# PV of a unit and scores of the next in one place on TensorE, with q/k transposes two units ahead

## The chip, the cores and the metric

The kernel runs on one core of a Trainium2 chip. The metric is device time in microseconds of one execution; lower is better. The engines are named as the profile names them: PE (TensorE matmul; PEld its weight loads), ACT (ScalarE), DVE (VectorE), POOL (GpSimd), SP (SyncE, which here only issues DMAs).

## What is computed

Chunked attention, then a two-layer network on the 4608 tokens that it gives. Batch 8, 8 heads, sequence 576, head size 64; attention stays inside chunks of 64 tokens.

```python
scores = scale * np.matmul(q_c, k_c.transpose(0, 1, 2, 4, 3))   # per chunk of 64
attn = np.exp(scores - max); attn = attn / (sum(attn) + 1e-09)
x = np.matmul(attn, v_c)              # -> x: 4608 tokens x 512
h = x @ w_in                          # 512 -> 2048
g = h * (1.0 / (1.0 + np.exp(-beta * h)))
out = g @ w_out                       # 2048 -> 512, float32
```

## The kernel before, in words

**Tiling.** The 4608 tokens are cut into 18 units of 256 tokens (four chunks, all heads) and 9 blocks of two units (512 tokens). Block j holds units 2j and 2j + 1. Matrices are in fp16, sums in fp32 PSUM.

**A unit's way.** `load_unit` has POOL issue the DMAs of q, k and v (fp32 in DRAM, converted on the way). `emit_T(u)` brings k and q into the layout with head size on partitions; from unit 8 on (`XU = 8`) these are two DMA transposes issued by SP (L149), before that transposes on DVE. `emit_T` also asks for the loads of unit u + 4 (`loads_to`), whose q and k go into the four-buffer pool `qk` that this T reads. `emit_sc(u)` puts the scores into the two banks of the PSUM pool `ps_s` with 32 small matmuls (64 x 64, four at a time on the array; L218) and ACT takes their exponential (L224). `emit_pv(u)` makes the product with v, the sum of the exponentials as a 65th column, in two halves of 16 small matmuls (L256): half 0 in `ps_x`, half 1 in `ps_s`. `emit_norm(u, s)` divides on DVE (reciprocal L267, multiply L271), and `emit_xt_dma(u, s)` has SP transpose the half into the block's tile `xt` (L292).

**A block's two layers.** `emit_m(j, m)`, m from 0 to 15, is one slice of the first layer: four matmuls of 512 columns into one bank of `ps_p` called `hps` (L303), then tanh on ACT (L313) and a multiply-add on DVE (L317) that writes `gt`. It reads the whole `xt` tile of its block, all four transposed halves. `emit_t(j, t, k0, k1)` is the second layer for 128 tokens: 16 matmuls of 512 columns into one bank called `ops` (L335), in two halves of eight; after the second, ACT copies it out (L345) and SP issues the DMA to DRAM (L347).

**PSUM.** Eight banks: four in `ps_p`, handed out in turn, two in `ps_s`, two in `ps_x`.

**The order.** Nothing reorders instructions: the program runs under `tc.manual_schedule()`, and each engine executes in the order in which the code emits. SP and POOL are such queues too. Blocks 0 to 2 are written out by hand. For blocks 3 to 8 a list of items with due times is sorted: 16 `emit_m`, 8 halves of `emit_t` of the block before (j - 1), and the attention of the two units of the next block:

```python
items.append((0.98 * (t + 0.5 * hf) / 4, 1, ("t", t, hf)))
return [(a0, 2, ("sc", u)), (a0 + 0.40 * w, 3, ("pv", u)),
        (a0 + 0.41 * w, 3, ("norm", u, 0)), (a0 + 0.55 * w, 3, ("norm", u, 1)),
        (a0 + 0.10 * w, 3, ("T", u + 1))]
```

So a block begins with a half of `ops`, then two `hps`, then the next half of `ops`, and so on; scores of a unit, its PV and the scores of the next unit stand at three different places among them, and the transposes of unit u + 1 follow the scores of unit u. In the profile of before, block 3 begins at 97.27 us, block 4 at 126.83, block 8 at 245.04.

Of the kernel before, what the change touches and what calls it, by code (L numbers as in the profile page):

```python
# [8 lines left out]
FP32 = mybir.dt.float32  # L9
FP16 = mybir.dt.float16  # L10
ACTF = mybir.ActivationFunctionType
ALU = mybir.AluOpType
# [3 lines left out]
def kernel(  # L16
# [10 lines left out]
    nc = tc.nc  # L27
    B, H, S, D = q.shape
# [4 lines left out]
    KFF = DFF // 128  # L33
    UNIT = 256
    NU = NT // UNIT
# [4 lines left out]
    const = ctx.enter_context(tc.tile_pool(name="const", bufs=1))  # L40
    big = ctx.enter_context(tc.tile_pool(name="big", bufs=1))
    qk_p = ctx.enter_context(tc.tile_pool(name="qk", bufs=4))
    qt_p = ctx.enter_context(tc.tile_pool(name="qt", bufs=2))
    et_p = ctx.enter_context(tc.tile_pool(name="et", bufs=3))
    rd_p = ctx.enter_context(tc.tile_pool(name="rd", bufs=2))
    x_p = ctx.enter_context(tc.tile_pool(name="x16", bufs=4))
# [4 lines left out]
    ps_p = ctx.enter_context(tc.tile_pool(name="ps_p", bufs=4, space=bass.MemoryType.PSUM))  # L51
    ps_s = ctx.enter_context(tc.tile_pool(name="ps_s", bufs=1, space=bass.MemoryType.PSUM))
    ps_x = ctx.enter_context(tc.tile_pool(name="ps_x", bufs=1, space=bass.MemoryType.PSUM))
# [112 lines left out]
    et_t = {}  # L166
# [39 lines left out]
    def emit_ex(u):  # L206
        ex_t[u].pop(0)()

    def emit_sc(u, split=False, later=False):
        qt, kt = qT.pop(u), kT.pop(u)  # L210
        sc = ps_s.tile([128, 2, H, CH], FP32, tag="s", name="sc")
        if u >= XU:
            qx, kx = (t.rearrange("p h s e -> p (h s e)").rearrange("p (j c t) -> p j c t", j=H, c=2)
                      for t in (qt, kt))
            for jj in range(H):
                for par in range(2):
                    for c in range(2):
                        nc.tensor.matmul(  # L218
                            out=sc[64 * c:64 * c + 64, par, jj, :],
                            lhsT=kx[64 * par:64 * par + 64, jj, c, :],  # L220
                            rhs=qx[64 * par:64 * par + 64, jj, c, :],
                        )
            et = et_p.tile([128, 2, H, CH], FP16, tag="et", name="et")
            nc.scalar.activation(out=et, in_=sc, func=ACTF.Exp, scale=scale)  # L224
            et_t[u] = et
            return
        for h in range(H):
            for e in range(2):
                for c in range(4):
                    p0, o0 = 32 * c, 64 * (c % 2)  # L230
                    nc.tensor.matmul(  # L231
                        out=sc[o0:o0 + 64, c // 2, h, :],
                        lhsT=kt[p0:p0 + 32, h, :, e],
                        rhs=qt[p0:p0 + 32, h, :, e],
                        start=(e == 0),
                        stop=(e == 1),
                    )
        et = et_p.tile([128, 2, H, CH], FP16, tag="et", name="et")
        ex_t[u] = [
            lambda s=s: nc.scalar.activation(out=et[:, s], in_=sc[:, s], func=ACTF.Exp, scale=scale)  # L240
            for s in ([0, 1] if split or later else [slice(0, 2)])
        ]
        et_t[u] = et
        while ex_t[u] and not later:
            emit_ex(u)

    def emit_pv(u):
        et = et_t.pop(u)
        for s in range(2):
            i = 2 * u + s  # L250
            pool, tag = ((ps_x, "x"), (ps_s, "s"))[s]
            x = pool.tile([128, 2, 4, 128], FP32, tag=tag, name="x")
            for g in range(4):
                for r in range(2):
                    for c in range(2):
                        nc.tensor.matmul(  # L256
                            out=x[64 * c:64 * c + 64, r, g, 0:D + 1],
                            lhsT=(et[64 * r:64 * r + 64, s, 4 * c + g, :] if u < XU else
                                  et[64 * r:64 * r + 64, g % 2, 4 * s + 2 * c + g // 2, :]),
                            rhs=vbig[64 * r:64 * r + 64, i, 4 * c + g, 0:D + 1],  # L260
                        )
            x_t[u, s] = x

    def emit_norm(u, s):
        x = x_t.pop((u, s))
        rd = rd_p.tile([128, 2, 4, 1], FP32, tag="rd", name="rd")
        nc.vector.reciprocal(out=rd, in_=x[:, :, :, D:D + 1])  # L267
        x16 = x_p.tile([128, 2, 4, D], FP16, tag="x16", name="x16")
        for r in ([0, 1] if u < 2 else [slice(0, 2)]):
            o = x16[:, r]  # L270
            nc.vector.tensor_tensor(  # L271
                out=o, in0=x[:, r, :, 0:D], in1=rd[:, r].to_broadcast(list(o.shape)), op=ALU.mult
            )
        x16_t[u, s] = x16
# [15 lines left out]
    def emit_xt_dma(u, s):  # L290
        xf = x16_t.pop((u, s)).rearrange("p r h d -> p (r h d)")
        nc.sync.dma_start_transpose(out=xt_at(u, s), in_=xf)  # L292
# [3 lines left out]
    def emit_m(j, m, c0=0, n=None, later=False):  # L296
        n = blocks[j][1] * UNIT if n is None else n
        if j not in gt_t:
            gt_t[j] = gt_p.tile([128, KFF, 512], FP16, tag="gt", name="gt")
        hps = ps_p.tile([128, 512], FP32, tag="p", name="hps")  # L300
        xr = xt_t[j].rearrange("p t (r k) (c q) -> p (t r) (k c) q", r=2, c=2)
        for kk in range(KDM):
            nc.tensor.matmul(  # L303
                out=hps[:, 0:n],
                lhsT=w_in16[m // 2][:, kk, (m % 2) * 128:(m % 2) * 128 + 128],
                rhs=xr[:, c0 // CH:(c0 + n) // CH, 2 * (kk % 2) + kk // 2, :],
                start=(kk == 0),
                stop=(kk == KDM - 1),
            )
        sg = sg_p.tile([128, 512], FP32, tag="sg", name="sg")  # L310

        def act():
            nc.scalar.activation(  # L313
                out=sg[:, 0:n], in_=hps[:, 0:n], func=ACTF.Tanh, scale=beta2[:, m:m + 1])

        def vec():
            nc.vector.scalar_tensor_tensor(  # L317
                out=gt_t[j][:, m, c0:c0 + n], in0=sg[:, 0:n], scalar=1.0, in1=hps[:, 0:n],
                op0=ALU.add, op1=ALU.mult,
            )  # L320

        if later:
            return act, vec
        act()
        vec()
# [3 lines left out]
    def emit_t(j, t, k0=0, k1=None):  # L329
        k1 = KFF if k1 is None else k1  # L330
        if k0 == 0:
            ops_t[j, t] = ps_p.tile([128, DM], FP32, tag="p", name="ops")
        ops = ops_t[j, t]
        for kk in range(k0, k1):
            nc.tensor.matmul(  # L335
                out=ops,
                lhsT=gt_t[j][:, kk, t * 128:(t + 1) * 128],
                rhs=w_out16[kk // 4][:, kk % 4, :],
                start=(kk == 0),
                stop=(kk == KFF - 1),  # L340
            )
        if k1 < KFF:
            return
        osb = osb_p.tile([128, DM], FP32, tag="osb", name="osb")
        nc.scalar.activation(out=osb, in_=ops, func=ACTF.Copy, scale=0.5)  # L345
        r0 = blocks[j][0] * UNIT + t * 128
        nc.sync.dma_start(out=out[r0:r0 + 128, :], in_=osb)  # L347
# [6 lines left out]
    with tc.manual_schedule():  # L354
# [149 lines left out]
                emit_xt_dma(7, 1)  # L504
                loads_to(11)

        def att_items(u, a0, w):
            return [(a0, 2, ("sc", u)), (a0 + 0.40 * w, 3, ("pv", u)),
                    (a0 + 0.41 * w, 3, ("norm", u, 0)), (a0 + 0.55 * w, 3, ("norm", u, 1)),
                    (a0 + 0.10 * w, 3, ("T", u + 1))]  # L510

        for j in range(3, NB):
            items = [(0.02 + 0.98 * m / KFF, 0, ("m", m)) for m in range(KFF)]
            for t in range(4):
                for hf in range(2):
                    items.append((0.98 * (t + 0.5 * hf) / 4, 1, ("t", t, hf)))
            if j + 1 < NB:
                for i in range(2):
                    items += att_items(2 * j + 2 + i, 0.03 + 0.43 * i, 0.43)
            items.sort(key=lambda it: it[:2])  # L520
            for _, _, it in items:
                if it[0] == "m":
                    emit_m(j, it[1])
                elif it[0] == "t":
                    emit_t(j - 1, it[1], 8 * it[2], 8 * it[2] + 8)
                elif it[0] == "sc":
                    emit_sc(it[1])
                elif it[0] == "pv":
                    emit_pv(it[1])
                elif it[0] == "norm":  # L530
                    emit_norm(it[1], it[2])
                    emit_xt_dma(it[1], it[2])
                elif it[1] < NU:
                    emit_T(it[1])
        for t in range(3):
            emit_t(NB - 1, t)
        for hf in range(2):
# [47 lines left out]
```

The softmax here doesn't subtract the row's maximum and nothing guards it: scores larger than these inputs give would overflow.

## Time and profile before

| | |
|---|---|
| median of 3 runs | 291.93 us (291.70 to 292.49) |
| the profiled execution | 291.74 us, span 290.0 us |
| PE busy | 283.1 us (98%), granted clock 1.0 |
| ACT / DVE busy | 146.0 us (50%) / 139.8 us (48%) |
| first layer, PE L303 | 608 matmuls, mean 368 ns |
| second layer, PE L335 | 560 matmuls, mean 379 ns |
| DMA queue of POOL, q0 | 101216 packets, 18.10 MB |
| DMA queue of SP, q1 | 40544 packets, 18.24 MB |
| unit's load of q (128 KB a DMA), issue to landing | median 6.6 us |
| transposes of k / q from unit 8 on, issue to landing | median 7.2 / 9.8 us |
| transposes into xt, issue to landing | median 3.5 us |

The span runs from the first to the last instruction; the time of an execution has 1.7 us more around it. Ends of matmuls are modelled and overlap the next one's start, so PE's pace is read from starts: eight matmuls of 512 columns take 1.727 us from start to start. Busy shares are means over the span; what an edit is worth is read at its own place in the timeline.

### The profile page before, as it was taken

How to read it: one execution, taken by the hardware profiler on the slowest of the kernel's cores; microseconds unless marked ns; L12 is line 12 of the kernel's file. 1: busy time of each engine (PE TensorE's matmuls, PEld its weight loads, DVE VectorE, ACT ScalarE, POOL GpSimd, SP SyncE). 2: the span in 40 equal slices, each digit the busy share in tenths (PEclk: the TensorE clock that was granted, in tenths of full speed). 3: DMA queues.
4: the chain of work that ended last, by engine and by line, in shares of the span. 5: the costliest groups of instructions: out<-in, count | busy, mean ns of one | idle time of the engine just before them, and what ended most of it. 6: DMA issues, size and time to landing. Idle time of an engine off the chain costs nothing.

```text
span 290.0 us, 6476 instructions
## 1 busy us (share of the span) xinstructions
PE 283.1 (98%) x2695; PEld 135.5 (47%) x2695; DVE 139.8 (48%) x252; ACT 146.0 (50%) x224; POOL 97.5 (34%) x126
## 2 busy tenths in 40 slices
PE   7999999999999999999999999999999999999995
PEld 2464445545544444444444444444444444444444
DVE  3477444687366644534454444445453636433300
ACT  3277318783456645454545554455445544444411
POOL 8864569379152985070717070000000000000000
PEclk9999999999999999999999999999999999999999
DMA  9999999999969999999999999946346202100111
GB/s 143 170 196 205 177 176 212 211 161 158 133 98 135 200 168 144 168 151 156 135 123 171 118 158 113 198 65 92 91 107 78 75 36 72 38 36 36 38 72 72
DMA packets 141932, 36.86 MB, mean 127 GB/s; under 512 B 130000, under 2 KB 137424, under 8 KB 141904
## 3 DMA queue, kind: packets, MB, share of 16 engines
q0 software_dynamic: 101216, 18.10, 84.2%
q1 hardware_dynamic: 40544, 18.24, 34.4%
q8 instruction: 21, 0.34, 0.5%
q10 hardware_dynamic: 144, 0.13, 0.1%
q14 instruction: 7, 0.06, 0.1%
HBM read 36.71 MB, written 9.44 MB: 159 GB/s over the span
## 4 chain that ended last, share of the span: by engine, by line
PE 91%; DMA 2%; ACT 2%; DVE 2%; POOL 1%; issue 1%; DVEq 0%; ACTq 0%; POOLq 0%
PE hps L303 43%; PE ops L335 41%; DMA ku<-in_k_dram 2%; PE x L256 2%; PE sc L231 2%; PE sc L218 1%; PE ops L540 1%; ACT xt L288 1%; DVE x L271 1%; ACT sg L313 1%; PE warm L352 1%; POOL h L360 1%; PE xp L287 1%; DVE kT L154 0%; ACT osb L345 0%
## 5 line engine op out<-in xcount | busy, mean ns | idle before, releaser
L317 DVE SCALAR_TENSOR_TENSOR gt<-sg,hps 128x512 f16<-128x512 f32 (+1 forms) x152 | 99.2, 658 | 114.5 <-ACT sg L313 114.4
L313 ACT ACTIVATE sg<-hps,beta 128x512 f32<-128x512 f32 (+1 forms) x152 | 100.4, 665 | 74.7 <-PE hps L303 74.7
L303 PE MATMUL hps<-xt,win 128*128 128x512 f16 (+1 forms) x608 | 136.7, 368 | 0.4 <-ACT xt L288 0.2
L335 PE MATMUL ops<-wout,gt 128*128 128x512 f16 x560 | 131.1, 379 | 0.0
L303 PEld LDWEIGHTS <-win 128*128 128x128 f16 x608 | 57.6, 98 | 61.8 <-issue 0.9
L335 PEld LDWEIGHTS <-gt 128*128 128x128 f16 x560 | 53.8, 98 | 63.3
L345 ACT ACTIVATE osb<-ops 128x512 f32<-128x512 f32 x35 | 20.9, 598 | 44.4 <-PE ops L335 44.4
L110 POOL DMA_DIRECT2D vbig<-in_v_dram x40 | 34.2, 876 | 10.0 <-DMA wout<-in_moe_w_out_dram 4.3
L96 POOL DMA_DIRECT2D qu<-in_q_dram x22 | 18.7, 860 | 41.5 <-DMA qT<-qu 39.0
L271 DVE TENSOR_TENSOR x<-x,rd 128x512 f16<-128x512 f32 (+1 forms) x40 | 25.2, 637 | 1.4
L96 POOL DMA_DIRECT2D ku<-in_k_dram x22 | 18.8, 876 | 0.4 <-DMA ku<-in_k_dram 0.4
L240 ACT ACTIVATE et<-sc 128x1024 f16<-128x1024 f32 (+1 forms) x9 | 7.4, 834 | 10.2 <-PE sc L231 10.2
L352 PE MATMUL warm<-idle 128*128 128x512 f16 x39 | 11.2, 429 | 1.2 <-DVE braw L356 1.2
L267 DVE RECIPROCAL rd<-x 128x8 f32<-128x8 f32 x36 | 7.2, 200 | 8.8 <-PE x L256 8.8
L224 ACT ACTIVATE et<-sc 128x1024 f16<-128x1024 f32 x10 | 10.2, 1015 | 0.0
L256 PEld LDWEIGHTS <-et 64*64 64x64 f16 x576 | 6.1, 107 | 7.4 <-issue 3.8
L102 POOL DMA_DIRECT2D ku<-in_k_dram x10 | 7.7, 772 | 2.5 <-DMA win<-in_moe_w_in_dram 1.3
L102 POOL DMA_DIRECT2D qu<-in_q_dram x10 | 7.7, 781 | 2.4 <-DMA win<-in_moe_w_in_dram 1.4
L288 ACT COPY xt<-xp 128x512 f16<-128x512 f16 x12 | 6.7, 588 | 3.3 <-PE xp L287 3.3
L256 PE MATMUL x<-vbig,et 64*64 64x65 f16 x576 | 8.1, 195 | 0.0
L154 DVE STREAM_TRANSPOSE kT<-ku 128x512 f32<-128x512 f32 x7 | 5.0, 711 | 4.9 <-DMA ku<-in_k_dram 4.9
L553 DVE TENSOR_SCALAR osb<-ops 128x256 f32<-128x256 f32 x1 | 0.4, 424 | 12.5 <-PE ops L540 12.5
(34 smaller groups left out, 60.2 us busy)
## 6 DMA issues: line engine op xcount, KB each, us to landing
out_dram<-osb SPq DMA_DIRECT2D x35, 256.0 KB, 3.2
vbig<-in_v_dram POOLq DMA_DIRECT2D x32, 128.0 KB, 7.9
qu<-in_q_dram POOLq DMA_DIRECT2D x20, 128.0 KB, 6.6
ku<-in_k_dram POOLq DMA_DIRECT2D x20, 128.0 KB, 8.2
win<-in_moe_w_in_dram POOLq DMA_DIRECT2D x8, 256.0 KB, 9.2
wout<-in_moe_w_out_dram POOLq DMA_DIRECT2D x4, 512.0 KB, 12.2
qu<-in_q_dram POOLq DMA_DIRECT2D x4, 256.0 KB, 6.5
ku<-in_k_dram POOLq DMA_DIRECT2D x4, 256.0 KB, 7.3
```

What stands on the lines that cost most here:

```text
L96: nc.gpsimd.dma_start(out=tv[off:off + n, sp], in_=src[b, :, s:s + n, :].rearrange("h p d -> p h d"),)
L102: nc.gpsimd.dma_start(out=t[off // 2:(off + n) // 2], in_=src[b, :, s:s + n, :].rearrange("h (p r) d -> p h r d", r=2),)
L110: nc.gpsimd.dma_start(out=vbig[off:off + n, i, :, 0:D], in_=v[b, :, s:s + n, :].rearrange("h p d -> p h d"),)
L224: nc.scalar.activation(out=et, in_=sc, func=ACTF.Exp, scale=scale)
L256: nc.tensor.matmul(out=x[64 * c:64 * c + 64, r, g, 0:D + 1], lhsT=(et[64 * r:64 * r + 64, s, 4 * c + g, :] if u < XU else et[64 * r:64 * r ...
L271: nc.vector.tensor_tensor(out=o, in0=x[:, r, :, 0:D], in1=rd[:, r].to_broadcast(list(o.shape)), op=ALU.mult)
L303: nc.tensor.matmul(out=hps[:, 0:n], lhsT=w_in16[m // 2][:, kk, (m % 2) * 128:(m % 2) * 128 + 128], rhs=xr[:, c0 // CH:(c0 + n) // CH, 2 * ...
L313: nc.scalar.activation(out=sg[:, 0:n], in_=hps[:, 0:n], func=ACTF.Tanh, scale=beta2[:, m:m + 1])
L317: nc.vector.scalar_tensor_tensor(out=gt_t[j][:, m, c0:c0 + n], in0=sg[:, 0:n], scalar=1.0, in1=hps[:, 0:n], op0=ALU.add, op1=ALU.mult,)
L335: nc.tensor.matmul(out=ops, lhsT=gt_t[j][:, kk, t * 128:(t + 1) * 128], rhs=w_out16[kk // 4][:, kk % 4, :], start=(kk == 0), stop=(kk == K ...
L345: nc.scalar.activation(out=osb, in_=ops, func=ACTF.Copy, scale=0.5)
L352: nc.tensor.matmul(out=d[:, 0:w], lhsT=idle[:, 0:128], rhs=idle[:, 0:w])
```

## The change

From block 3 on the sorted list is replaced by a fixed order. In each of eight steps of a block come two `emit_m`, then, at some steps, a "hop" of attention work, then a half of `emit_t` of the block before. Block 3 has the hops scores 8, PV 8, scores 9, PV 9, scores 10 (steps 0, 2, 3, 5, 6). Blocks 4 to 7 have two hops each (steps 0 and 4): hop u is PV of unit u and, right behind it, the scores of unit u + 1. Block 8 has none. PV of these hops is done by a new function `emit_pv_p`: its first half stays in `ps_x`, its second half goes into two banks of `ps_p` (called y) instead of `ps_s`; `emit_norm_p` divides the second half first, bank by bank, then the first. The transposes of q and k are issued at the scores of a unit for the unit two later (at the scores of unit 9 for units 10 and 11 together), ahead of the hop's own transposes into `xt`, and their pool has three buffers instead of two.

```diff
--- before.py
+++ after.py
@@ -40,7 +40,7 @@
     const = ctx.enter_context(tc.tile_pool(name="const", bufs=1))
     big = ctx.enter_context(tc.tile_pool(name="big", bufs=1))
     qk_p = ctx.enter_context(tc.tile_pool(name="qk", bufs=4))
-    qt_p = ctx.enter_context(tc.tile_pool(name="qt", bufs=2))
+    qt_p = ctx.enter_context(tc.tile_pool(name="qt", bufs=3))
     et_p = ctx.enter_context(tc.tile_pool(name="et", bufs=3))
     rd_p = ctx.enter_context(tc.tile_pool(name="rd", bufs=2))
     x_p = ctx.enter_context(tc.tile_pool(name="x16", bufs=4))
@@ -243,6 +243,37 @@
         et_t[u] = et
         while ex_t[u] and not later:
             emit_ex(u)
+
+    def emit_pv_p(u):
+        et = et_t.pop(u)
+        x = ps_x.tile([128, 2, 4, 128], FP32, tag="x", name="x")
+        y = [ps_p.tile([128, 4, 128], FP32, tag="p", name=f"y{r}") for r in range(2)]
+        for s in (1, 0):
+            for g in range(4):
+                for r in range(2):
+                    for c in range(2):
+                        nc.tensor.matmul(
+                            out=(y[r][64 * c:64 * c + 64, g, 0:D + 1] if s else
+                                 x[64 * c:64 * c + 64, r, g, 0:D + 1]),
+                            lhsT=et[64 * r:64 * r + 64, g % 2, 4 * s + 2 * c + g // 2, :],
+                            rhs=vbig[64 * r:64 * r + 64, 2 * u + s, 4 * c + g, 0:D + 1],
+                        )
+        x_t[u] = x, y
+
+    def emit_norm_p(u):
+        x, y = x_t.pop(u)
+        rd = rd_p.tile([128, 2, 4, 1], FP32, tag="rd", name="rd")
+        x16 = x_p.tile([128, 2, 4, D], FP16, tag="x16", name="x16")
+        for r in range(2):
+            nc.vector.reciprocal(out=rd[:, r], in_=y[r][:, :, D:D + 1])
+            nc.vector.tensor_tensor(
+                out=x16[:, r], in0=y[r][:, :, 0:D], in1=rd[:, r].to_broadcast([128, 4, D]), op=ALU.mult
+            )
+        x16_t[u, 1] = x16
+        emit_xt_dma(u, 1)
+        x_t[u, 0] = x
+        emit_norm(u, 0)
+        emit_xt_dma(u, 0)
 
     def emit_pv(u):
         et = et_t.pop(u)
@@ -504,34 +535,35 @@
                 emit_xt_dma(7, 1)
                 loads_to(11)
 
-        def att_items(u, a0, w):
-            return [(a0, 2, ("sc", u)), (a0 + 0.40 * w, 3, ("pv", u)),
-                    (a0 + 0.41 * w, 3, ("norm", u, 0)), (a0 + 0.55 * w, 3, ("norm", u, 1)),
-                    (a0 + 0.10 * w, 3, ("T", u + 1))]
-
         for j in range(3, NB):
-            items = [(0.02 + 0.98 * m / KFF, 0, ("m", m)) for m in range(KFF)]
-            for t in range(4):
-                for hf in range(2):
-                    items.append((0.98 * (t + 0.5 * hf) / 4, 1, ("t", t, hf)))
-            if j + 1 < NB:
-                for i in range(2):
-                    items += att_items(2 * j + 2 + i, 0.03 + 0.43 * i, 0.43)
-            items.sort(key=lambda it: it[:2])
-            for _, _, it in items:
-                if it[0] == "m":
-                    emit_m(j, it[1])
-                elif it[0] == "t":
-                    emit_t(j - 1, it[1], 8 * it[2], 8 * it[2] + 8)
-                elif it[0] == "sc":
-                    emit_sc(it[1])
-                elif it[0] == "pv":
-                    emit_pv(it[1])
-                elif it[0] == "norm":
-                    emit_norm(it[1], it[2])
-                    emit_xt_dma(it[1], it[2])
-                elif it[1] < NU:
-                    emit_T(it[1])
+            if j == 3:
+                hops = {0: "s8", 2: "v8", 3: "s9", 5: "v9", 6: "s10"}
+            elif j == NB - 1:
+                hops = {}
+            else:
+                hops = {0: f"m{2 * j + 2}", 4: f"m{2 * j + 3}"}
+            for i in range(8):
+                emit_m(j, 2 * i)
+                emit_m(j, 2 * i + 1)
+                if i in hops:
+                    how, u = hops[i][0], int(hops[i][1:])
+                    us = {"s": u, "v": NU, "m": u + 1}[how]
+                    if how == "v":
+                        emit_pv(u)
+                    if how == "m":
+                        emit_pv_p(u)
+                    if us < NU:
+                        emit_sc(us)
+                    for ut in {"s8": [9], "s9": [10, 11], "v8": [], "v9": []}.get(hops[i], [us + 2]):
+                        if ut < NU:
+                            emit_T(ut)
+                    if how == "v":
+                        for sp in range(2):
+                            emit_norm(u, sp)
+                            emit_xt_dma(u, sp)
+                    if how == "m":
+                        emit_norm_p(u)
+                emit_t(j - 1, i // 2, 8 * (i % 2), 8 * (i % 2) + 8)
         for t in range(3):
             emit_t(NB - 1, t)
         for hf in range(2):
```

## The prediction

> **What bounds the kernel now.** I read the page's forty slices first. TensorE (PE) stands at 9 from the second slice on at full clock, so every microsecond saved or lost on PE is one of the span. The DMA row is the second thing to see: it too stands at 9 until slice 26 (about 188 us), so until then the DMA engines have little to spare.
>
> ```profile
> PE   7999999999999999999999999999999999999995
> DMA  9999999999969999999999999946346202100111
> ```
>
> Then the timeline of PE. Around one score site:
>
> ```profile
> 198.98 1.89 PE L303 MATMUL hps<-xt,win 128*128 128x512 f16 x8
> 200.80 0.45 PE L218 MATMUL sc<-qT,kT 64*64 64x64 f16 x32
> 201.18 1.90 PE L335 MATMUL ops<-wout,gt 128*128 128x512 f16 x8
> ```
>
> Eight large matmuls take 1.727 us from start to start (215.49 to 217.21 elsewhere in this view), so without the site the next line would start at 200.71; it starts at 201.18. A site of 32 small matmuls costs 0.48 us; PV sites (206.46, 222.10) cost the same. Single starts inside the site come in fours, 32 ns a four, so 8 x 0.032 = 0.26 us is the work and 0.22 us is going in (0.09) and out (0.13). Around the start of block 3, PE does the second layer first:
>
> ```profile
> 97.27 1.89 PE L335 MATMUL ops<-wout,gt 128*128 128x512 f16 x8
> 99.00 1.03 PE L303 MATMUL hps<-xt,win 128*128 128x512 f16 x4
> ```
>
> What feeds that L303 comes through SP's queue. Its timeline (start, time in SP's hands):
>
> ```profile
> 92.36 2.63 SPq L292 DMA_TRANSPOSE xt<-x  x2
> 95.15 1.56 SPq L149 DMA_TRANSPOSE kT<-ku  x1
> 96.81 1.52 SPq L149 DMA_TRANSPOSE qT<-qu  x1
> ...
> 107.62 3.84 SPq L292 DMA_TRANSPOSE xt<-x  x2
> 111.55 0.55 SPq L347 DMA_DIRECT2D out_dram<-osb  x1
> 112.27 1.34 SPq L149 DMA_TRANSPOSE kT<-ku  x1
> 113.72 5.88 SPq L149 DMA_TRANSPOSE qT<-qu  x1
> 119.69 0.53 SPq L347 DMA_DIRECT2D out_dram<-osb  x1
> 121.53 2.68 SPq L292 DMA_TRANSPOSE xt<-x  x2
> ```
>
> The view of one tile gives issue to landing. For the two xt of unit 7 (92.4 and 93.8) and for the qT of unit 10 (113.7):
>
> ```profile
> DMA to landing us min/median/max: 4.7/4.8/5.0
> DMA to landing us min/median/max: 11.1/11.1/11.1
> ```
>
> So xt of unit 7 is complete at 93.80 + 4.7 = 98.5, and T(10), my name for unit 10's k and q transposes, at 113.72 + 11.1 = 124.8. Last, the DMA view of 126.4 to 139.4, in which one unit's loads (POOL's queue q0) and T(11) (SP's q1) run together:
>
> ```profile
> q0 software_dynamic: 6240, 0.79, 123.0%
> q1 hardware_dynamic: 2897, 1.16, 55.7%
> ```
>
> SP's queue moves 1.16 MB in 13 us there. In 112 to 124 it is 1.19 in 12, in 141 to 154 1.23 in 13: together 0.094 MB/us beside loads. From 185.5 to 191.3, with no loads, it is 0.92 in 5.8, 0.159 MB/us.
>
> **The Trainium skill.** "TensorEngine Tiling (Array Packing)", Key Properties: changing the tiling mode drains TensorE. The trace agrees, with the 0.22 us above. "DMA: Bandwidth & Descriptors", Queues, rings and completion order: each DMA engine takes a ring's descriptors in order. The trace agrees as far as it goes: the output issued at 111.55 lands 8.0 us later at 119.5, after the xt issued at 110.27 (117.7, 7.4 us) and before T(10). Same page, Issuing engines are not separate DMA queues: SP's and POOL's transfers share 16 engines. It agrees: 0.094 against 0.159 MB/us. "TensorE: Matmul & The Clock Gate", Part 1: an idle window of about 3.4 us halves the clock. No run here shows it; this trace has no such gap.
>
> **The change, part by part.** The sum is made against the profiled execution: span 290.0, time 291.74, 0.2 under the median of 291.93.
>
> *Merging sites.* Before, units 8 to 17 have 20 sites: 9.60 us. After, five single ones in block 3, seven merged ones (PV 10 to 16 with scores 11 to 17), one PV alone. A merged site has 16 fours: 0.22 + 0.51 = 0.736 us. Sum 6 x 0.48 + 7 x 0.736 = 8.03. **Gain 1.57 us**, all on PE's path.
>
> *PV's second half in ps_p banks.* Two of the four rotating banks serve y once per unit. Counting the rotation (h h y y o h h h h o h h per half block), the next hps that needs a y bank comes 3.3 us after the site begins; y is normalised 2.3 to 2.9 us after it (a gt 0.69 that ends 1.65 us in, two reciprocals of 0.20, two half multiplies of some 0.4). No wait. The tight one is ops: it takes the bank of the first hps, free 1.65 us after that hps ends (tanh 185.27, gt ends 186.68), and is wanted after 0.86 + 0.09 + 0.64 = 1.6 us. I take 0.1 us each, eight times: **0.8 us**; between 0 and 1.6. VectorE's extra reciprocal and split multiply, some 0.3 us a unit, cost nothing beside its 48%; without that cover they would hold ops by as much.
>
> *hps pair ahead of the half ops.* In block 3 the first hps now comes at 97.27, but it reads the xt tile that is complete at 98.5. Before, the ops half (1.73 us) covered this. PE is in order, so everything behind it waits: **1.25 us**. Nothing ahead of block 3 is changed, so I hold this to be near certain.
>
> *T two units ahead.* Each T puts two DMAs of 0.26 MB on SP's queue; the numbers of DMAs stay, their places move. In block 3, T(10) and T(11) both come at the scores of unit 9, ahead of the output of tile 1 and of xt(9). Before, T(11) was issued at 126.43, after xt(9) had landed (126.4). What is late next:
> - T(10): that output now comes after it. It took 1.8 us of the queue (117.7 to 119.5), so T(10) lands near 123.0. The scores of unit 10 are due at 97.27 + 1.25 + 13 x 1.727 + 4 x 0.48 = 122.9. Wait 0.1; if T(10) lands as before, 1.9.
> - xt(9), wanted by the first hps of block 4, has T(11), an output and itself to move from 123.0: 0.52 + 0.26 + 0.26 = 1.05 MB. The loads of unit 14 wait for T(10) (POOL's idle 12.7 us ends on it), so some 2.5 us go at 0.159 (0.40 MB), the rest at 0.094: 6.9 us. It lands at 132.4. Block 4 is due at 97.27 + 1.25 + 16 x 1.727 + 5 x 0.48 = 128.6. **Wait 3.8 us**; between 2 and 6.5.
> - xt(11), for block 5: ahead of it now stand T(12), T(13), xt(10), T(14) and four outputs, since T(u+2) is issued ahead of xt(u). With itself 1.57 + 0.52 + 1.05 = 3.15 MB at 0.094: 33.4 us, so 165.8. Loads stay beside it throughout: units 15, 16, 17 start as T(11), T(12), T(13) land, and units 14 to 17 are 4 x 0.79 MB at 0.06 MB/us, 50 us and more. Block 4 takes 27.63 + 2 x 0.736 + 0.2 = 29.3, so block 5 is due at 161.7. **Wait 4.1 us**; between 0 (if q1 keeps more than 0.107 MB/us) and 10 (if it has to wait out the loads of unit 17).
> - Later, no loads are left: xt lands in 2.4 to 3 us, and T(15) to T(17) have ten and more to spare.
> POOL's loads themselves come earlier and cost PE nothing but this. The order at the end (ops half after the last hps pair) moves no work: 0.
>
> Sum: 1.25 + 0.1 + 3.8 + 4.1 + 0.8 - 1.57 = **+8.4 us**, span 298.4, time **300.1**.
>
> **Rivals.**
> *One wait only:* SP's queue recovers in block 4, xt(11) is in time: 300.1 - 4.1 = 296.0. For it: T's land steadily in 10 to 11 us in every unit of the trace of before, no backlog grows. Against: there each T had 14.7 us to itself, here four share some 40.
> *No queue at all (the other side):* the transposes of T(10) and T(11), alone on the rings, pass at the rate without loads: T(11) and xt(9) in 1.05/0.159 = 6.6 us from T(10), which itself lands by 122, so at 128.6; block 5 in time. Left are 1.25 + 0.0 to 0.8 - 1.57: 291.4 to 292.2, no change. It decides at xt(9) landing by 128.6 and xt(11) by 161.7. Against it: T(11)'s real price beside a load was 12.7 us.
> *Heavier:* xt(11) waits out unit 17's loads, or a wait of about 4 us spans an idle window of the clock and the next 3.4 us run at half speed (estimate from the clock page: 1.7 us each): 303 to 307.
> *Merging does nothing:* PE drains between PV and scores too: every case 1.6 us more.
>
> **How the numbers follow.** Two waits 0.45, one wait 0.33, heavier 0.14, no queue 0.08. The time is that of the likeliest, 300.1, whose own range is 297 to 303. The range of 293.5 to 305.5 takes in one wait with a short one (xt(9) two microseconds sooner) and part of the heavier. A measurement of this kernel tells about 0.3%, 0.9 us, from no change: faster 0.03 (only if the 1.25 us wait is absent as well), same 0.06, slower 0.91.
>
> **What would show it.** First hps of block 3 at 98.5 with an idle PE before it, released by the xt DMA; idle PE of some 4 us before block 4 and again before block 5, each ended by xt; qT(11) landing near 129 and xt(9) after it; merged sites of 0.73 us; from block 6 on no idle. I am wrong if xt(9) lands ahead of T(11), if the idle time before blocks 4 and 5 is under 1 us together, or if merged sites cost 0.95.

## The result and the profile after

The changed kernel takes 299.14 us (median of 6 runs, 297.88 to 301.77) against 292.03 (291.70 to 292.49) for the kernel before on the same chip: ratio 1.0254, 95% interval 1.0209 to 1.0299. It is slower by 7.1 us; 8.2 were forecast over the median. Ratios, here and below, leave out runs more than 1.5% above the fastest of the same kernel: two of the four of the third experiment, the profiled one among them, and one of the 22 of the ninth. The profiled execution is one of 298.55 us with a span of 296.8, so the two profiles differ by 6.8 us.

From the page of the changed kernel, the same two rows of slices:

```profile
PE   7899999999999899959998899999999999999995
DMA  9999999999989999999999995151112120101111
```

PE no longer stands at 9 throughout: there are dips in slices 14, 18 and 22 to 23 (numbered from 1; 7.42 us each), that is near 98 and 130 us and between 156 and 171. DMA falls off two slices earlier than before: the loads are done sooner.

The groups by line, with all releasers, say what the first layer waited for (columns after the bar: busy time and mean ns; then idle time before it in us and who ended it):

```profile
L334 PE MATMUL hps<-xt,win 128*128 128x512 f16 (+1 forms) x608 | 134.9, 368 | 6.4 <-DMA xt<-x 3.1 <-issue 1.9 <-DVE gt L348 1.0
```

Before, this group had 0.4 us of idle time. The timeline of PE puts the 6.4 us in their places; the bracket is idle time and what ended it:

```profile
93.83 4.26 PE L334 MATMUL hps<-xt,win 128*128 128x512 f16 x19
99.08 1.89 PE L334 MATMUL hps<-xt,win 128*128 128x512 f16 x8 [0.99 <-DVE gt L348]
...
124.03 0.45 PE L218 MATMUL sc<-qT,kT 64*64 64x64 f16 x32 [0.41 <-DMA qT<-qu]
...
127.87 1.89 PE L366 MATMUL ops<-wout,gt 128*128 128x512 f16 x8
132.87 1.89 PE L334 MATMUL hps<-xt,win 128*128 128x512 f16 x8 [3.11 <-DMA xt<-x]
134.68 0.32 PE L255 MATMUL y<-vbig,et 64*64 64x65 f16 x16
134.83 0.30 PE L255 MATMUL x<-vbig,et 64*64 64x65 f16 x16
134.96 0.49 PE L218 MATMUL sc<-qT,kT 64*64 64x64 f16 x32
135.39 1.89 PE L366 MATMUL ops<-wout,gt 128*128 128x512 f16 x8
...
160.36 1.89 PE L366 MATMUL ops<-wout,gt 128*128 128x512 f16 x8
164.18 1.89 PE L334 MATMUL hps<-xt,win 128*128 128x512 f16 x8 [1.92 <-issue]
```

Measured start to start, less the usual pace, the waits are 1.14, 0.48, 3.27 and 2.08 us: before block 3, before the scores of unit 10, before blocks 4 and 5. The bracket at 99.08 names DVE and that at 164.18 "issue", but the transposes say otherwise: xt(7), issued at 94.46, lands 4.5 us later at 99.0, and xt(11), issued at 156.89, 7.2 later at 164.1. Where the releaser named had long been free, the landing has to be looked up. From block 6 on no wait for a transfer is left.

SP's queue in block 3, to be held against the one shown before:

```profile
110.67 2.53 SPq L323 DMA_TRANSPOSE xt<-x  x2
113.37 2.47 SPq L149 DMA_TRANSPOSE kT<-ku  x1
115.94 4.45 SPq L149 DMA_TRANSPOSE qT<-qu  x1
120.57 2.23 SPq L149 DMA_TRANSPOSE kT<-ku  x1
122.96 1.23 SPq L149 DMA_TRANSPOSE qT<-qu  x1
124.30 0.52 SPq L378 DMA_DIRECT2D out_dram<-osb  x1
124.92 2.60 SPq L323 DMA_TRANSPOSE xt<-x  x2
```

xt(9) stands behind T(10) and T(11). Its second half, issued at 126.22, lands 6.5 us later at 132.7, and PE goes on at 132.87. Meanwhile POOL issues the loads of unit 14 as soon as T(10) has landed, and those of unit 15 right behind them:

```profile
124.44 1.75 POOL L96 DMA_DIRECT2D qu<-in_q_dram  x2 [11.71 <-DMA qT<-qu]
126.16 1.77 POOL L96 DMA_DIRECT2D ku<-in_k_dram  x2
127.89 1.80 POOL L110 DMA_DIRECT2D vbig<-in_v_dram  x2
129.63 2.30 POOL L96 DMA_DIRECT2D qu<-in_q_dram  x3
```

**The sum.** The waits add up to 6.97 us. The places of attention work among the large matmuls took 20 x 0.48 = 9.60 before. Now there are five of 0.48, seven merged ones of 0.79 (the ops behind them starts 2.52 us after the first hps of the step, 132.87 to 135.39, less 1.727) and one PV alone, also of 0.79: 8.72. That is 0.88 gained, so 6.09 lost. The other 0.66 lies ahead of the change: block 3 was due at 97.93 instead of 97.27, as unit 1's scores came 0.5 us later at the start of the program (11.48 against 10.98), where nothing is changed. This is chance: in the profiles of the experiments below, which are alike up to there, block 3 is due between 96.99 and 98.03.

### The profile page after: what moved, and what is told of

Read it like the earlier page. It is cut to its first block, busy times and chain, and to the rows that moved or that the text cites. A ratio compares the mean times of both kernels' runs of the same rounds, so it can differ in the third digit from the quotient of the medians.

```text
span 296.8 us, 6491 instructions
## 1 busy us (share of the span) xinstructions
PE 282.8 (95%) x2695; PEld 136.0 (46%) x2695; DVE 142.3 (48%) x268; ACT 147.4 (50%) x224; POOL 97.4 (33%) x126
## 4 chain that ended last, share of the span: by engine, by line
PE 65%; DMA 18%; POOL 8%; DVE 3%; ACT 2%; issue 2%; SPq 0%; POOLq 0%; DVEq 0%; ACTq 0%
PE ops L366 30%; PE hps L334 30%; DMA qu<-in_q_dram 8%; POOL qu L96 3%; DMA vbig<-in_v_dram 3%; DMA qT<-qu 3%; DMA xt<-x 2%; POOL vbig L110 2%; DMA ku<-in_k_dram 2%; POOL ku L96 2%; PE sc L231 1%; ACT sg L344 1%; PE ops L572 1%; DVE x L302 1%; ACT xt L319 1%
## 5 line engine op out<-in xcount | busy, mean ns | idle before, releaser
L334 PE MATMUL hps<-xt,win 128*128 128x512 f16 (+1 forms) x608 | 134.9, 368 | 6.4 <-DMA xt<-x 3.1
L334 PEld LDWEIGHTS <-win 128*128 128x128 f16 x608 | 58.7, 98 | 71.4 <-issue 8.3
L366 PEld LDWEIGHTS <-gt 128*128 128x128 f16 x560 | 53.2, 98 | 62.0 <-issue 0.2
L302 DVE TENSOR_TENSOR x<-x,rd 128x512 f16<-128x512 f32 (+1 forms) x32 | 19.6, 624 | 1.1
L298 DVE RECIPROCAL rd<-x 128x8 f32<-128x8 f32 x28 | 5.6, 199 | 9.4 <-PE x L287 9.4
L269 DVE TENSOR_TENSOR x<-y,rd 128x256 f16<-128x256 f32 x16 | 6.8, 425 | 0.5
L128 POOL DMA_DIRECT2D win<-in_moe_w_in_dram x8 | 6.0, 756 | 1.5 <-DMA vbig<-in_v_dram 1.4
```

Of the source, the lines that this page charges most:

```text
L302: nc.vector.tensor_tensor(out=o, in0=x[:, r, :, 0:D], in1=rd[:, r].to_broadcast(list(o.shape)), op=ALU.mult)
L334: nc.tensor.matmul(out=hps[:, 0:n], lhsT=w_in16[m // 2][:, kk, (m % 2) * 128:(m % 2) * 128 + 128], rhs=xr[:, c0 // CH:(c0 + n) // CH, 2 * ...
L366: nc.tensor.matmul(out=ops, lhsT=gt_t[j][:, kk, t * 128:(t + 1) * 128], rhs=w_out16[kk // 4][:, kk % 4, :], start=(kk == 0), stop=(kk == K ...
```

## The experiments

The expectations call the first run e1_gate, the fourth e4, the fifth e5_gate_best, the sixth e6_split, the ninth e9_gate_on_xt. The theory: the waits for xt come from the DMA engines, which loads pulled forward and transposes pulled forward now share in the same 30 us. The first rival: the order on SP's queue alone. First, the loads of units 14 to 17 held back, nothing else moved: `emit_gate` has POOL copy one column of the normalised half, and the loads stand behind this copy on POOL.

```diff
-        if which[-1] == "qT" and u not in (6, 7, 8):
+        if which[-1] == "qT" and u not in (6, 7, 8) and u < 10:
             loads_to(u + 4)
...
         x16_t[u, 1] = x16
+        emit_gate(u)            # emit_norm_p
...
                         emit_norm_p(u)
+                        loads_to(u + 4)
```

> The changed kernel, with the loads of units 14 to 17 held back on POOL until the second PV half of units 10 to 13 is normalised; nothing else moved. Theory (POOL's loads and SP's transposes share the DMA engines, and the loads pulled forward slow T(11), xt(9) and what stands before xt(11)): xt(9) lands near 127.5 instead of 132.7, the wait of 3.3 us before block 4 falls under 0.5, that of 2.1 before block 5 under 1; the 1.15 us before block 3 and the 0.4 before the scores of unit 10 stay. Time 293 to 294.5. Rival (the order on SP's queue alone is to blame, T(11) ahead of xt(9)): the waits stay within 1 us of 3.3 and 2.1, time 298 to 300.

293.09 us, ratio 1.0048 (1.0031 to 1.0065): 6 us back. In its timeline of PE:

```profile
121.17 1.89 PE L335 MATMUL hps<-xt,win 128*128 128x512 f16 x8
124.90 0.45 PE L218 MATMUL sc<-qT,kT 64*64 64x64 f16 x32 [1.84 <-DMA qT<-qu]
...
128.74 1.89 PE L367 MATMUL ops<-wout,gt 128*128 128x512 f16 x8
130.47 1.89 PE L335 MATMUL hps<-xt,win 128*128 128x512 f16 x8
```

The order on SP's queue is that of the changed kernel, yet block 4 begins without a wait, and block 5 too. The second half of xt(9), issued at 126.79, lands after the first of these times; in the changed kernel, issued at 126.22, it took the second:

```profile
DMA to landing us min/median/max: 2.4/2.4/2.4
```

```profile
DMA to landing us min/median/max: 6.5/6.5/6.5
```

The order alone is refuted. Only the wait for T(10) is longer here (1.9 us): it lands at 124.8 instead of 123.9. The held-back loads have no part in that, since neither kernel issues a load of units 14 to 17 before T(10) has landed.

Second, the order alone:

```diff
-  {"s8": [9], "s9": [10, 11], ...}
+  {"s8": [9], "s9": [10], ...}          # and emit_T(11) behind xt(9)
```

> The changed kernel, with T(11) alone moved behind xt(9) on SP's queue. Theory (DMA capacity between 122 and 135 us is short whatever stands first): xt(9) lands near 127 and the wait before block 4 goes, but then the scores of unit 11, right behind the first hps pair of block 4, wait for T(11), which beside the loads of unit 14 needs some 12 us and lands at 136 to 138: a wait of 4 to 6 us there, time 298 to 302. Rival (order alone): 3.3 us gained, 295.5 to 296.5.

296.88 us, ratio 1.0185 (1.0137 to 1.0233). The median lies between the two ranges expected, but the interval overlaps that of the changed kernel (1.0209 to 1.0299): how much is gained stays open. xt(9) now lands 2.5 us after issue and block 4 begins in time, but T(11)'s qT, issued at 125.88, takes 8.4 us beside the loads of unit 14:

```profile
130.88 0.30 PE L255 MATMUL x<-vbig,et 64*64 64x65 f16 x16
134.41 0.65 PE L218 MATMUL sc<-qT,kT 64*64 64x64 f16 x32 [3.24 <-DMA qT<-qu]
134.99 3.60 PE L366 MATMUL ops<-wout,gt 128*128 128x512 f16 x8
138.38 2.73 PE L334 MATMUL hps<-xt,win 128*128 128x512 f16 x8
```

The wait of 3.3 us has gone from one transfer to another, as the theory has it, shorter than the 4 to 6 forecast. Two other waits are shorter in this profile: that for T(10) is gone, because this execution landed it at 123.2, and block 5's is 1.5 instead of 2.1. The profile is of the slowest of the four runs, 300.07 us; the others took 295.98 to 297.02. The last two lines show a second thing: after the wait, eight matmuls take 3.4 us instead of 1.73. The table of windows gives the granted clock:

```profile
129.00:133.00 4.00, 2.18 (x41) 1.00 1.74 116
135.00:139.00 4.00, 4.00 (x15) 0.50 1.62 176
```

(Columns: window, its length, PE busy and instructions, clock, DMA share, GB/s.) During the idle time of 3.2 us the granted clock fell to half. Behind it twelve starts of large matmuls lie 0.43 instead of 0.216 us apart, and the scores take 0.58 instead of 0.38 us: 2.7 us lost beside the wait.

Third and fourth: half ops ahead of the hps pair again, alone and with the loads held back. The merged places then have to be at odd steps: at even ones their y banks would take in turn the bank of the ops that is only half summed.

```diff
             for i in range(8):
+                emit_t(j - 1, i // 2, 8 * (i % 2), 8 * (i % 2) + 8)
                 emit_m(j, 2 * i)
...
-                emit_t(j - 1, i // 2, 8 * (i % 2), 8 * (i % 2) + 8)
...
-                hops = {0: f"m{2 * j + 2}", 4: f"m{2 * j + 3}"}
+                hops = {1: f"m{2 * j + 2}", 5: f"m{2 * j + 3}"}
```

> The changed kernel, with each half ops put ahead of the hps pair again, as before, and for the banks' sake the merged places one step later (steps 1 and 5). Theory (block 5 begins when xt(11) lands, and that is set by the DMA queue, not by PE): the 1.15 us before block 3 goes; the first hps of block 4 and of block 5 still come near 132.8 and 164, with one half ops (1.73 us) already done, so 1.7 us in all is gained: 297 to 298. Rival (each wait stands by itself and is covered by a half ops): 1.15 + 1.73 + 1.73 gained, 294.5.

303.69 us, ratio 1.031 (1.0265 to 1.0355, from 299.86 and 302.35). Both expectations were wrong. The wait before block 3 did go, but those before blocks 4 and 5 grew in the profile:

```profile
134.13 3.60 PE L334 MATMUL hps<-xt,win 128*128 128x512 f16 x8 [4.83 <-DMA xt<-x]
...
170.87 3.38 PE L334 MATMUL hps<-xt,win 128*128 128x512 f16 x8 [4.56 <-DMA out_dram<-osb]
```

My picture of block 5, that the DMA queue sets its start whatever PE does, was false. The merged place came 7.5 us later (156.8 against 149.3): 3.45 because it stands a step later, 1.26 because block 4 began later, 2.79 because PE ran at half clock behind the wait. So xt(11) was issued 6.6 later (163.5 against 156.9) and landed 6.5 later (170.6). The chain runs from the place through the norm to the transfer, and the queue adds its 7 us to it. The profiled execution took 305.04 us and has the halved clock behind both waits, so their sizes are those of this execution alone; without the 2.8 us the place would still be 4.7 us late.

> Both: loads of units 14 to 17 held back, and the half ops ahead of the hps pair with the merged places at steps 1 and 5. Theory: no wait for xt is left, only about 0.4 us before the scores of unit 10; against the kernel before, merging (0.9 us by the sites of the profile after) is left: ratio 0.996 to 1.000, time 290.8 to 292.0. Rival (merging brings nothing, or the banks y wait again at the new place): 292.5 to 294.

294.65 us, ratio 1.0093 (1.0078 to 1.0109): above both ranges. Waits of 0.5, 1.4 and 1.5 us are left before blocks 4, 5 and 6. The loads were released by the same norm as xt, and met it: xt of unit 11 took 5.3 and 6.6 us.

Fifth to seventh, with the places at steps 1 and 3 and the scores of unit 10 at step 7: what merging is worth.

```diff
-                hops = {1: f"m{2 * j + 2}", 5: f"m{2 * j + 3}"}
+                hops = {1: f"m{2 * j + 2}", 3: f"m{2 * j + 3}"}
...                                       # sixth and seventh: scores a step later
+                if hops.get(i - 1, "")[:1] == "m" and int(hops[i - 1][1:]) + 1 < NU:
+                    emit_sc(int(hops[i - 1][1:]) + 1)
...                                       # seventh: old halves of PV
-                        emit_pv_p(u)
+                        emit_pv(u)
```

> Loads of units 14 to 17 held back and half ops ahead of the hps pair, as in the fourth run, but the merged places at steps 1 and 3 instead of 1 and 5, so that xt of a block's second unit is issued some 7 us earlier, and the scores of unit 10 at step 7 instead of 6. Theory (in the fourth run xt of the second unit, issued at 152.5 and 153.7, met the loads released at the same moment and landed at 160.3, late by 1.4): no wait for a transfer is left, the merging's 0.9 us are: 290.8 to 291.6, ratio 0.996 to 0.999. Rival (loads released twice in 7 us now delay both): waits of 1 to 2 us before blocks 5 and 6 again, 292.5 to 295.

> The same as e5_gate_best, but the scores of unit u + 1 stand one step behind PV of unit u instead of right behind it; PV's second half stays in the y banks. Theory (ops behind a PV place is held to 2.5 us from the first hps's start by its bank, so PV alone costs 0.79 as the last one of the changed kernel did, and a separate scores place 0.48): 7 x 0.48 = 3.4 us more than e5_gate_best. Rival (a separate place costs only its going in and out, 0.22): 1.6 us more.

> The same as e6_split, but PV as in the kernel before, its second half in ps_s, no y banks. Two places of 0.48 against one of 0.79: 7 x 0.17 + (0.48 - 0.79) = 0.9 us more than e5_gate_best, about the time of the kernel before. If merging is worth the 0.22 us a place of the prediction with no bank wait: 1.5 us more.

Measured: 293.13 (ratio 1.0045, 1.0029 to 1.0061), 295.31 (1.0115, 1.0099 to 1.0131), 294.68 (1.0100, 1.0083 to 1.0116). For the fifth the rival held: waits of 0.3, 0.7 and 1.5 us before blocks 4 to 6. The medians of the three can't all be set against each other, since the profile of the sixth has 0.4 us of such waits and the others 2.5 and 2.6. The profiles can be, from the time at which block 3 was due (98.03, 97.08, 97.59) to the end of the span (292.4, 292.8, 292.9) and less these waits: 191.9, 195.3 and 192.7 us. So the sixth takes 3.4 and the seventh 0.8 us more than the fifth, where 3.4 and 0.9 had been expected; the kernel before takes 192.7, as the seventh. By their medians the seventh is 1.5 us behind the fifth, whose profiled run is its slowest; the part beyond 0.8 is not shown by a profile. The sixth kernel, PV into the y banks and scores apart:

```profile
132.30 1.89 PE L335 MATMUL hps<-xt,win 128*128 128x512 f16 x8
134.12 0.32 PE L255 MATMUL y<-vbig,et 64*64 64x65 f16 x16
134.27 0.30 PE L255 MATMUL x<-vbig,et 64*64 64x65 f16 x16
134.83 1.89 PE L367 MATMUL ops<-wout,gt 128*128 128x512 f16 x8 [0.26 <-DVE gt L349]
```

From 132.30 to 134.83 is 2.53 us again, with half as much in the place: PV alone costs 0.80, since ops waits for the bank that gt frees. A merged place has 0.74 us of work of its own and so hides nearly all of that wait. The price of the y banks is seen only where merging doesn't cover it.

Eighth, the kernel before with only the hps pair ahead of the half ops:

```diff
-  items.append((0.98 * (t + 0.5 * hf) / 4, 1, ("t", t, hf)))
+  items.append((0.09 + 0.98 * (t + 0.5 * hf) / 4, 1, ("t", t, hf)))
```

> The kernel before, with only the hps pair ahead of the half ops in blocks 3 to 8 (the due time of the halves moved by 0.09); attention, transposes and loads as before. Theory: one wait of 1.2 us before block 3, nothing later, as xt of the later blocks landed 0.5 to 1.5 us ahead of their start: 292.9 to 293.4. Rival (the shift is absorbed by a later wait, or each block start waits as well): 292.0, or over 294.

293.21 us, ratio 1.0043 (1.0031 to 1.0055), 1.2 us more than before, and its profile has a single wait, before block 3:

```profile
95.78 1.67 PE L303 MATMUL hps<-xt,win 128*128 128x512 f16 x7
98.55 1.02 PE L303 MATMUL hps<-xt,win 128*128 128x512 f16 x4 [1.10 <-DVE gt L317]
```

The last three look for a version that keeps the merging without the waits.

```diff
+                        if u + 4 < NU:                # ninth: loads behind xt's landing
+                            nc.gpsimd.tensor_copy(out=gate, in_=xt_at(u, 0)[:, 0, 0:1])
+                            loads_to(u + 4)
...
                         emit_norm_p(u)
+                        if us + 2 < NU:               # eleventh: T behind xt on SP's queue
+                            emit_T(us + 2)
```

> The changed kernel with half ops ahead of the hps pair, merged places at steps 1 and 5, the scores of unit 10 at step 7, and the loads of units 14 to 17 released only when the hop's own transposes into xt have landed (POOL copies one column of xt first). Theory (in the fourth and fifth run loads released together with xt slowed it: issue to landing 5 to 8 us against 2.5 alone): xt lands in 2.5 to 4 us, no wait for a transfer from block 4 on, only the merging's 0.9 us are left: 290.8 to 291.6. Rival (loads later now make T(14) to T(17) late, and xt stands behind them on SP): waits of 1 to 2 us before blocks 5 and 6, 292.5 to 295.

> The first run (e1_gate: order of the changed kernel, loads held back until the second PV half is normalised) with the scores of unit 10 one step later, at step 7 of block 3. Theory: T(10) lands near 125 as in e1_gate, the scores are now due at 126.4, so the 1.9 us wait of e1_gate goes; the 0.9 to 1.2 before block 3 stays; xt(9) lands near 129.2, block 4 is due near 129.5: 291.2 to 291.9. Rival (the wait only moves on to block 4 or to the scores of unit 11): 292.7 to 293.5.

> e9_gate_on_xt with the transposes of q and k of a merged place issued after its two transposes into xt instead of ahead of them. Theory (the one wait left in e9_gate_on_xt, 1.1 us before block 6, comes from xt(13) standing behind T(16) on SP's ring; q and k are needed a place later and have the time): no wait for a transfer from block 3 on, 290.8 to 291.4, ratio 0.996 to 0.999. Rival (the loads, gated on xt, then meet T, and T comes late for the scores of the next place but one, or a wait of 1 us stays before block 6): 291.9 to 292.6.

The ninth takes 292.12 us, ratio 1.0012 (0.9998 to 1.0025): as fast as before by the median, though five of its 22 runs are slower than any of the kernel before. Its profile has one wait of 1.1 us before block 6; behind T(16) there, xt(13) lands 2.4 us after an issue that itself came late. The tenth takes 292.59, ratio 1.0024 (1.0016 to 1.0033), between its two ranges: the 1.9 us wait is gone and none followed it to block 4, but that before block 3 was 1.7 in the profiled run, more than forecast. The eleventh takes **291.02 us, ratio 0.9976 (0.9968 to 0.9984)**, faster than both kernels and within the theory's range. Its first layer waits no longer from block 3 on, save 0.4 us before block 4:

```profile
L334 PE MATMUL hps<-xt,win 128*128 128x512 f16 (+1 forms) x608 | 134.9, 368 | 0.8 <-DMA xt<-x 0.4 <-ACT xt L319 0.3
```

and xt lands, from 130 to 200 us, in these times (first the eleventh kernel, then the changed one):

```profile
DMA to landing us min/median/max: 2.4/3.4/4.2
```

```profile
DMA to landing us min/median/max: 2.4/6.2/8.3
```

## Why the prediction was right

- **The direction and its cause.** Waits before blocks 3, 4 and 5 ended by xt, none later, a small one before the scores of unit 10: all four are in the timeline. The first and eighth run show two of the causes by themselves.
- **The size.** The terms of the forecast add up to 8.48, not 8.4; measured in the profile, the same terms are 6.09. That the time came within 1 us of 300.1 is in part luck: the profiled execution began block 3 0.66 us late, and four of the six runs had a lower granted clock.
- **hps pair ahead, 1.25 us.** Measured 1.14, and 1.2 alone in the eighth run.
- **T(10), 0.1 us.** Measured 0.48; qT(10) landed at 123.9 where 123.0 was worked out. In the first two runs it landed at 124.8 and 123.2, so this term moves by more than its size from execution to execution.
- **xt(9), 3.8 us, landing at 132.4.** Measured 3.27, landing at 132.7. The total is right and its parts are not. T(11) passed faster than thought: it landed at 126.1, 2.2 us after T(10), before a load was moving, as the rival of no queue had it. Then xt(9) took some 6 us for a quarter of a megabyte beside the loads. The DMA view of 122 to 126 us, then that of 126 to 133 (packets, MB):

```profile
q1 hardware_dynamic: 2914, 0.91, 120.9%
q0 software_dynamic: 27, 0.00, 1.3%
```

```profile
q0 software_dynamic: 3770, 0.48, 124.3%
q1 hardware_dynamic: 1233, 0.52, 49.4%
```

So q1 moved 0.23 MB/us instead of 0.159, then 0.074 instead of 0.094, and the two errors cancelled by luck. With the same order on SP's queue and no load beside it (first run) xt(9) landed in 2.4 us: the loads arriving together with xt weighed more than what stood ahead of it.

- **xt(11), 4.1 us.** Measured 2.08, the mis-sized term. q1 moved 3.21 MB from 132.7 to 164.1, as much as counted (3.15), at 0.102 instead of 0.094 MB/us; 31.4 us instead of 33.4. The third run showed this step's picture incomplete as well: it holds only while the merged place comes early enough.
- **Merging, 1.57 less 0.8 for the banks.** 0.88 measured. The banks cost about 0.05 at a merged place and 0.3 at the last PV alone, 0.7 in all.
- **The heavier rival.** The clock did not halve in the profiled execution. The six runs' mean granted clock goes from 1.0 (297.88 and 298.55 us) over 0.993 (298.73) and 0.994 (299.55, 300.46) to 0.989 (301.77), and the second run shows the half clock behind a wait of such a length, at 2.7 us where 1.7 was estimated. That part of the spread fits it; no profile of the changed kernel itself with a halved clock was taken.
- **The Trainium skill.** "DMA: Bandwidth & Descriptors", Issuing engines are not separate DMA queues, has all transfers run on the same 16 DMA engines, whichever engine issues them. The forecast rested most on this, and the first run bears it out: 2.4 us for xt(9) without POOL's loads, 6.5 beside them. "TensorE: Matmul & The Clock Gate", Part 1, has the clock halve after an idle window of about 3.4 us. In the second run less was enough: PE's last matmul ended near 131.2, and the granted clock is 1.00 in the window from 132.2 to 133.2 and 0.50 from 133.3 to 134.3. There the measurement decides. In the changed kernel's profile 3.1 us of idle time left the clock whole; what tells the two apart is not shown.

## What to carry to other kernels

Count what a queue has to move between two instants that the main engine can't shift, at the rate the queue reaches beside the other traffic, before pulling transfers forward: "earlier" for one is "behind" for another. The releases that follow are part of the move: here a transpose that lands sooner frees a load sooner, and that load meets the next transfer which the matmuls wait for. With the half ops ahead again, the urgent transfers first and the loads released by their landing, a kernel with the same merging, which had come with 7 us of loss, ran 0.24% faster than the kernel before. Of these moves only one was tried by itself, T behind xt on SP's queue (ninth run to eleventh); the third buffer of the pool for the q and k transposes was not.

## What had not been expected of the hardware

Beside a burst of loads SP's transfers don't keep a fixed share: 0.23 MB/us from 122 to 126 us before a load was moving, 0.074 from 126 to 133 as two units' loads begin, 0.102 on average after that. And a wait of 3.2 us on TensorE cost its length nearly twice in the profile of the second run, as twelve large matmuls behind it ran at 0.43 us. The rival had named such a loss; that the clock would fall some 2.1 us into the wait had not been expected.
